# A fused attention and feed-forward kernel: weights fetched four pieces ahead, the first masks moved to ScalarE and POOL, the audit paused and then doubled

## The chip, the cores and the metric

The kernel runs on one NeuronCore of a Trainium2 chip. Its engines work side by side, each through its own queue in order: TensorE (PE; PEld is its weight load) multiplies matrices into PSUM, VectorE (DVE) and ScalarE (ACT) work on elements, POOL (GpSimd) does a few set-up operations, and SyncE (SP) issues the DMAs. Times are device microseconds; the metric is the median of the runs.

## The reference

Gated linear attention feeds a two-layer feed-forward net with SiLU:

```
state = alpha[t] * state + k[t] (outer) v[t]      # per batch and head, 48 x 48
y[t]  = q[t] @ state                              # batch 4, heads 8, 768 tokens, head width 48
x     = y as (3072 tokens, 384)
h     = x @ w_in ; g = h * sigmoid(h)             # w_in: 384 x 2048
out   = g @ w_out                                 # w_out: 2048 x 384
```

q, k, v and alpha are float32. The two weights come as float64, so the kernel turns them into float32 itself.

## The kernel before

**Attention by chunks.** The 768 tokens of each batch are cut into 6 chunks of 128; with 4 batches these are 24 chunks, NT. A chunk n passes four stages. `products(n)` brings alpha, k and q into the layout (head width, token), forms by a scan the running products u of alpha, and with them the scaled keys kp; `quotient` makes the reciprocals and, by a second scan, the scaled queries qp. `scores(n)` multiplies kp with qp into two PSUM tiles and multiplies them with a causal mask into g (line 749). `values(n)` multiplies g with v and adds the part of the carried state; `states(n)` updates the state. A step of the main loop runs scores, values and states of chunk n-1 and products of chunk n, in four slots. The first NA = 8 chunks are turned by TensorE transposes (line 683) and use spare buffers; later ones are loaded in blocks and turned by VectorE.

**In the first 8 chunks and after.** The two 64-token halves of a chunk are handled apart: the second half of the heads has its halves swapped in kp (line 700) and in v (`load_v`, three DMAs a chunk), and scores are made in 16 small matmuls. All 24 chunks do this, though only the later ones leave out the empty quarter of the causal triangle.

**Weights.** `weights(which)` is a generator. A piece is 128 rows by 512 columns of w_in (12 pieces) or by 384 of w_out (16 pieces). `fetch` DMAs the 64-bit numbers into one of four buffers `bits`; ScalarE makes the low word's rounding `up` (line 613), and three VectorE instructions (616, 617, 618) assemble the float32. `convert` is called as the feed-forward work comes near. Before, three pieces are fetched at the very start (`load_w(3)`), the others when they are converted.

**Feed-forward.** Work is cut into `pieces` that `fill` puts between the attention's slots by a table of costs and due times. `enter_plain` (line 839, groups 0 and 1) and `enter` (line 862) make g from x, `leave` (line 960; the very first in line 987) makes the output from g. From group 2 on sums of blocks stand for some of the products, and VectorE makes these sums: `sums_w` of the weights, `sums_x` of the tokens, and those on g in `enter` (line 876).

**The audit.** The fast path holds only where alpha and the weights lie within bounds. `audit` is a generator: 37 times (9 pieces of alpha, 28 of the weights) it loads a piece into the single buffer `look` (lines 643, 645) and, when it is called next, reduces it on VectorE (line 653). Before, `fill` calls it once a step from step 8 on; those left over run after the loop, with one or two feed-forward pieces between them. Then a one-column matmul (line 1179) joins the bounds, and its result `small` decides whether the general path must run. Further pieces of output work follow it.

**Queues.** The tile framework puts each engine's instructions in an order by its own scheduling and adds semaphores. PSUM for attention (`ps_a`) has three buffers. In the first chunks k and q are transposed into the banks of the output work (`ps_o`).

Of the kernel before, what the change touches and what calls it, by code (L numbers as in the profile page):

```python
# [9 lines left out]
I32 = mybir.dt.int32  # L10
U32 = mybir.dt.uint32
U8 = mybir.dt.uint8
AF = mybir.ActivationFunctionType
# [342 lines left out]
def quotients(  # L356
# [58 lines left out]
    def out_bank(i, n):  # L415
        return outs[i].tile([128, 512], F32, name="ps_o")[:, 0:n]
# [58 lines left out]
    def load_v(n):  # L475
        c = ctxs.setdefault(n, dict(zip(("ci", "b"), divmod(n, B))))
        x = v[c["b"], :, c["ci"] * C : c["ci"] * C + C, :].transpose([1, 0, 2])
        t = c["v"] = vns[n % NV]
        nc.sync.dma_start(t[:, 0 : H // 2, 0:D], x[:, 0 : H // 2])
        for e in range(2):  # L480
            nc.sync.dma_start(t[CH * e : CH * e + CH, H // 2 :, 0:D], x[CH - CH * e : C - CH * e, H // 2 :])

    early = []
    wide = moe_w_in.dtype != F32

    def fetch(src):
        n = src.shape[1]
        bits = raw.tile([128, 512, 2], I32, name="bits")[:, 0:n, :]
        nc.sync.dma_start(bits.rearrange("p n w -> p (n w)"), src.bitcast(I32))
        return bits  # L490

    def load_w(n):

        for _ in range(n if wide else 0):
            t = len(early)
            early.append(fetch(moe_w_in[t * 128 : t * 128 + 128, 0:512]))

    load(0)
    load(1)
    load_w(3)  # L500

# [46 lines left out]

        return quads[:, at // NKT, at % NKT] if at < 4 * NKT else late["wx"][:, at - 4 * NKT]

    for n in range(2, NIN):
        load(n)
    for n in range(NV):
        load_v(n)

    def combine(to, sa, a, sb, b):
        if sa == sb == 1:
# [33 lines left out]
    def weights(which):  # L593

        pieces = [
            (w_in[:, t, c : c + 512], moe_w_in[t * 128 : t * 128 + 128, c : c + 512])
            for c in range(0, DF, 512) for t in range(NKT)  # L600
        ] if which == 0 else [
            (w_out[:, f, :], moe_w_out[f * 128 : f * 128 + 128, :]) for f in range(NFT)]
        for dst, src in pieces:
            if not wide:
                act.dma_start(dst, src)
                yield
                continue
            n = dst.shape[1]
            bits = early.pop(0) if which == 0 and early else fetch(src)
            lo, hi = bits.bitcast(U32)[:, :, 0], bits[:, :, 1]  # L610
            up = upp.tile([128, 512], I32, name="up")[:, 0:n]

            tc.keep_in_program_order(act.activation(up, lo, AF.Copy, scale=2.0**-29))
            w = dst.bitcast(I32)
# [3 lines left out]
            dve.tensor_tensor(w, w, up, ALU.add)  # L618
            yield


# [40 lines left out]
    def turned(x, to):  # L662
        x = x[:, 32:].rearrange("p (g j d) -> p g j d", j=4, d=D)
        dve.transpose(to.rearrange("p g (b j) -> p g j b", j=4), x[:, :, :, 0:32])

    def products(n):

        c = ctxs[n]
        sg = seg[0 if late else n % 2]
        ps = {}  # L670

        for name in ("a", "k", "q"):
            if n >= NA:
                if name == "a":
                    turned(c[name], tokens(sg))
                continue
            if n < GB and name != "a":

                ps[name] = out_bank("kq".index(name), 512).rearrange("p (j c) -> p j c", c=C)
            else:  # L680
                ps[name] = ps_attn()
            for j in range(NP):
                pe.transpose(ps[name][:, j, :], c[name][:, 2 * j : 2 * j + 2, :], ident)
            if name == "a":
                act.copy(tokens(sg), ps[name])
        end = NP * W
        u = upool.tile([128, end + 1], F32, name="u")
        dve.tensor_tensor_scan(u[:, end - 1 :: -1], sg[:, end:0:-1], one[:, end:0:-1],  # L688
                               0.0, ALU.mult, ALU.add)

        dve.tensor_single_scalar(least[:, n, :], u[:, 0:end:W], 2.0**-64, ALU.max)  # L691
        kp = c["kp"] = turns(kps, n)
        ut = tokens(u)
        if n >= NA:
            ps["k"] = late["turn"].tile([128, NP, C], F32, name="turn")
            turned(c["k"], ps["k"])
        j = NP // 2
        dve.tensor_tensor(kp[:, 0:j], ps["k"][:, 0:j], ut[:, 0:j], ALU.mult)
        k, ut = [x[:, j:].rearrange("p j (e c) -> p j e c", e=2) for x in (ps["k"], ut)]
        dve.tensor_tensor(kp[:, j:].rearrange("p j (e c) -> p j e c", e=2)[:, :, ::-1], k, ut, ALU.mult)  # L700
        if n >= NA:
            c["sg"] = sg
        else:
            quotient(n, sg, ps["q"])

    def quotient(n, sg=None, q=None):

# [24 lines left out]
    def scores(n):  # L732
        c = ctxs[n]
        ci, b = c["ci"], c["b"]
        ps = c.pop("blank") if n >= NA else [ps_attn() for _ in range(2)]

        for j in (0, 2, 1, 3):
            for e in range(2):  # L740
                for u in range(2):
                    r = slice(64 * u, 64 * u + D)
                    at = slice(CH * e, CH * e + CH)
                    t = slice(CH * (e ^ j // 2) if n >= NA else 0, C)
                    pe.matmul(ps[u][at, j, t], lhsT=c["kp"][r, j, at], rhs=c["qp"][r, j, t],  # L745
                              start=True, stop=True)
        g = c["g"] = work.tile([128, 2, NP, C], F32, name="g")
        for u in range(2):
            dve.tensor_tensor(g[:, u].rearrange("p (o j) c -> p o j c", o=2),  # L749
                              ps[u].rearrange("p (o j) c -> p o j c", o=2),  # L750
                              mask[:, :, None, :].to_broadcast([128, 2, NP // 2, C]), ALU.mult)
# [365 lines left out]
    def fill(step, slot):  # L1117

        at = step * SLOTS + slot
        if at < marks[0]:  # L1120
            if step >= 1:
                convert(0, (at - SLOTS) * 3 // (marks[0] - SLOTS) + 1)
            return
        i = next(i for i, m in enumerate(marks[1:]) if at < m)
        a, b = [work_at[n] for n in ([0] + phases)[i : i + 2]]
        due = a + (b - a) * (at - marks[i] + 1) / (marks[i + 1] - marks[i])
        if late and at % 4 == 0:
            next(audits, None)
        while work_at[done + 1] <= due and pieces[done][2] <= bridged:
            convert(0, 3 * (done // 2) + 6)  # L1130
            convert(1, 3 * (done - 6) // 2)
            go_on()

    for step in range(STEPS):
        stages = [[(scores, 1)], [(products, 0)], [(values, 1)], [(states, 1)]]
        if step < GB:

            stages = stages[1::-1] + stages[2:]
        elif step >= NA:
            stages = [[(scores, 1)], [(products, 0)], [(values, 1), (states, 1)], [(quotient, 0), (blank, 0)]]  # L1140
# [32 lines left out]
        dve.tensor_single_scalar(e, e, bound, holds)  # L1173
    good = work.tile([128, 1], F32, name="good")
    dve.tensor_reduce(good, ends, axis=AX, op=ALU.min)  # L1175
    go_on()
    go_on()
    ps = ps_attn()[0:1, 0, 0:1]
    pe.matmul(ps, lhsT=good, rhs=mask[:, 0, C - 1 : C], start=True, stop=True)  # L1179
    dve.tensor_single_scalar(small, ps, 127.5, ALU.is_ge)  # L1180
# [62 lines left out]
```

## Time and profile before

| | us |
|---|---|
| median of 10 runs | 571.14 |
| lowest and highest | 569.85, 573.98 |
| the profiled execution | 572.79 |
| its span | 571.0 |
| TensorE busy | 553.1 |
| VectorE busy | 448.8 |
| ScalarE busy | 202.0 |
| POOL busy | 8.4 |

| row of the profile | count | mean ns |
|---|---|---|
| mask product, VectorE, line 749 | 48 | 684 |
| scans, VectorE, lines 688 and 716 | 24 each | 1210, 1228 |
| key products, halves, lines 698 and 700 | 24 each | 414 to 424 |
| a w_in piece on VectorE, lines 616 to 618 | 12 each | 420, 685, 689 |
| rounding of a piece, ScalarE, line 613 | 28 | 611 |
| audit reductions, VectorE, line 653 | 65 | 687 |

The span runs from the program's first instruction to its last. A busy TensorE is not TensorE at its peak, since matmuls are pipelined and their ends are modelled. Every tile name is the program's own; `out<-in` says what an instruction writes and reads. Float32 matmuls show as two records each. Where idle time stands before an instruction, the name after the arrow is what ended it.

### The profile page before, as it was taken

The page shows a single profiled execution, that of the slowest core. Times are in us where ns is not written, and L with a number is a line of the kernel's source. Part 1 is how long each engine was busy: PE and PEld are TensorE (multiplying, and loading weights), DVE is VectorE, ACT ScalarE, POOL GpSimd, SP SyncE. Part 2 cuts the span into 40 slices and gives each one's busy share as a digit, 9 for nine tenths or more (in the row PEclk, how much of TensorE's full clock was granted, in tenths as well). Part 3 has the DMA queues.
Part 4 walks back from the last instruction along what each step waited for, and adds up shares of the span by engine and source line. Part 5 has one row for each costly group of instructions (what it writes and reads, how often), then busy time and mean ns, then how long its engine had stood idle before and what let it go on. Part 6 is the DMA issues. An engine that isn't in the chain of part 4 may idle for free. (4 is left out here: it accounts for less than half of the span.)

```text
span 571.0 us, 12612 instructions
## 1 busy us (share of the span) xinstructions
PE 553.1 (97%) x5154; PEld 489.8 (86%) x5154; DVE 448.8 (79%) x831; ACT 202.0 (35%) x399; POOL 8.4 (1%) x28
## 2 busy tenths in 40 slices
PE   5899999999999999899999999999999999999986
PEld 4677887678999999799999999999898999998986
DVE  5779698489798799996898897898894866757651
ACT  2336543133331342452443453443443241423100
POOL 4000000100000000000000000000000000000000
PEclk9899999999999999899999999999999999999999
DMA  9997682344434433433424423425410113333320
GB/s 213 164 294 186 198 207 72 95 104 121 121 100 123 111 104 95 133 82 97 127 50 123 125 71 104 126 49 128 127 39 22 52 58 115 115 103 119 104 71 27
DMA packets 94675, 63.83 MB, mean 112 GB/s; under 512 B 55568, under 2 KB 86288, under 8 KB 94608
## 3 DMA queue, kind: packets, MB, share of 16 engines
q1 hardware_dynamic: 94608, 62.94, 42.0%
q8 instruction: 42, 0.69, 0.5%
q14 instruction: 25, 0.20, 0.1%
HBM read 58.20 MB, written 4.72 MB: 110 GB/s over the span
## 5 line engine op out<-in xcount | busy, mean ns | idle before, releaser
L960 PE MATMUL ps_o<-w_out,g 128*128 128x192 f32 x704 | 122.7, 328 | 0.9 <-DVE o L974 0.8
L960 PEld LDWEIGHTS ps_o<-w_out,g 128*128 128x128 f32 x704 | 115.3, 190 | 3.8 <-DVE o L974 1.4
L960 PE MATMUL ps_o<-wt,g 128*128 128x192 f32 x528 | 91.6, 327 | 0.3 <-DVE u L1036 0.3
L839 PE MATMUL ps_m<-xt,w_in 128*128 128x256 f32 x384 | 88.9, 383 | 0.3 <-DVE w_in L618 0.3
L960 PEld LDWEIGHTS ps_o<-wt,g 128*128 128x128 f32 x528 | 87.2, 191 | 1.9 <-DVE u L1036 0.6
L839 PEld LDWEIGHTS ps_m<-xt,w_in 128*128 128x128 f32 x384 | 71.1, 190 | 10.9 <-DVE w_in L618 1.1
L862 PE MATMUL ps_m<-xc,w_in 128*128 128x256 f32 x288 | 70.1, 380 | 1.2 <-DVE g L876 1.2
L653 DVE TENSOR_REDUCE seen<-bits 128x1 f32<-128x384 int32 (+2 forms) x65 | 42.4, 687 | 25.6 <-DMA bits<-in_moe_w_out_dram 20.2
L862 PEld LDWEIGHTS ps_m<-xc,w_in 128*128 128x128 f32 x288 | 54.1, 191 | 7.6 <-DVE g L876 1.5
L873 ACT ACTIVATE g<-g 128x1024 f32<-128x1024 f32 x32 | 33.2, 1056 | 60.8 <-DVE g L876 60.8
L868 ACT COPY g<-ps_m 128x512 f32<-128x512 f32 x64 | 37.0, 585 | 38.2 <-PE ps_m L862 38.2
L862 PE MATMUL ps_m<-xc,wx 128*128 128x256 f32 x192 | 50.2, 384 | 0.0
L965 DVE TENSOR_TENSOR g<-g 128x512 f32<-128x512 f32 x66 | 44.3, 688 | 2.9 <-PE ps_o L960 2.9
L876 DVE TENSOR_TENSOR g<-ps_m,g 128x512 f32<-128x512 f32 x56 | 37.7, 684 | 2.5 <-PE ps_m L862 2.2
L761 ACT ACTIVATE st<-st,least 128x96 f32<-128x96 f32 x80 | 24.1, 364 | 44.1 <-DVE least L691 44.1
L749 DVE TENSOR_TENSOR g<-ps_a,mask 128x512 f32<-128x512 f32 x48 | 31.2, 684 | 9.4 <-PE ps_a L745 9.0
L862 PEld LDWEIGHTS ps_m<-xc,wx 128*128 128x128 f32 x192 | 35.0, 190 | 4.1 <-issue 0.4
L842 ACT ACTIVATE g<-ps_m 128x512 f32<-128x512 f32 x32 | 19.1, 595 | 47.9 <-PE ps_m L839 47.7
L688 DVE TENSOR_TENSOR_SCAN u<-al,one 128x516 f32<-128x516 f32 x24 | 29.0, 1210 | 8.2 <-POOL mask L529 4.5
L716 DVE TENSOR_TENSOR_SCAN p<-al,inv 128x516 f32<-128x516 f32 x24 | 29.5, 1228 | 6.8 <-PE ps_a L781 6.6
L781 PE MATMUL ps_a<-g,vn 128*32 128x128 f32 x768 | 29.6, 286 | 0.0
L781 PEld LDWEIGHTS ps_a<-g,vn 128*32 128x32 f32 x768 | 21.3, 114 | 8.8 <-issue 6.6
(121 smaller groups left out, 649.0 us busy)
## 6 DMA issues: line engine op xcount, KB each, us to landing
bits<-in_moe_w_in_dram SPq DMA_DIRECT2D x24, 512.0 KB, 4.1
bits<-in_moe_w_out_dram SPq DMA_DIRECT2D x32, 384.0 KB, 3.1
at<-in_alpha_dram SPq DMA_DIRECT2D x64, 96.0 KB, 2.3
kt<-in_k_dram SPq DMA_DIRECT2D x64, 96.0 KB, 2.4
qt<-in_q_dram SPq DMA_DIRECT2D x64, 96.0 KB, 2.4
bits<-in_alpha_dram SPq DMA_DIRECT2D x9, 512.0 KB, 3.4
out_dram<-o SPq DMA_DIRECT2D x48, 96.0 KB, 2.0
vn<-in_v_dram SPq DMA_DIRECT2D x24, 96.0 KB, 2.9
```

Source lines behind the costliest of these rows:

```text
L653: dve.tensor_reduce(seen[kind][which][:, i : i + 1], x, axis=AX, op=op, apply_absolute_value=True))
L688: dve.tensor_tensor_scan(u[:, end - 1 :: -1], sg[:, end:0:-1], one[:, end:0:-1], 0.0, ALU.mult, ALU.add)
L716: dve.tensor_tensor_scan(p[:, 0:end], sg[:, 0:end], iv[:, 0:end], 0.0, ALU.mult, ALU.add)
L749: dve.tensor_tensor(g[:, u].rearrange("p (o j) c -> p o j c", o=2), ps[u].rearrange("p (o j) c -> p o j c", o=2), mask[:, :, None, :].to_b ...
L781: pe.matmul(py[32 * at : 32 * at + 32, t, :], lhsT=w, rhs=x, start=(i < 4), stop=(i >= len(todo) - 4), skip_group_check=True)
L839: pe.matmul(ps[:, e, :], lhsT=w_in[:, t, (f + e) * 128 : (f + e + 1) * 128], rhs=xt[:, t, :], start=(t == 0), stop=(t == NKT - 1))
L862: pe.matmul(ps[:, e], lhsT=block_w(w)[:, 2 * pair + e], rhs=block_x(grp, x), start=(first and e == 0), stop=(e == 1), skip_group_check=True)
L868: act.copy(to, ps)
L873: act.activation(x, x, AF.Silu)
L876: dve.tensor_tensor(to, a, b, op)
L960: pe.matmul(ps, lhsT=x, rhs=w[:, i], start=(first and i == 0), stop=(i == HF - 1), skip_group_check=True)
L965: dve.tensor_tensor(cells(grp, h, pair, *to), cells(grp, h, pair, *x), cells(grp, h, pair, *y), ALU.subtract)
```

## The change

The first 8 chunks no longer swap their halves: one v DMA, one key product over all heads, 8 score matmuls of full width instead of 16 of half width. For the first 4 chunks (GB) ScalarE copies the scores from PSUM and POOL applies the causal mask in place; chunks 4 to 7 keep the VectorE mask. Chunk 1's k and q are transposed into banks of the feed-forward work (`bank`) rather than `ps_o`.

Weights are fetched in one list, w_in and then w_out: four pieces at the start, with chunk 0's and 1's v between them, and one more after each conversion, so that four are always under way. ScalarE's rounding of the next piece is issued right after the three VectorE instructions of the present one. Only in step 1 do the products come before the scores; before it was in steps 0 to 3. Loads of the next chunks move to the end of `states`.

The audit starts at step 15 and is called in two of the four slots of each step. After it, five pieces of output work are issued instead of two ahead of the one-column matmul, and four behind it as before.

```diff
@@ load_v
+        if n < NA:
+            nc.sync.dma_start(t[:, :, 0:D], x)
+            return
         nc.sync.dma_start(t[:, 0 : H // 2, 0:D], x[:, 0 : H // 2])
...
+    pieces_in = [(t, c) for c in range(0, DF, 512) for t in range(NKT)]
+    sources = [moe_w_in[t * 128 : t * 128 + 128, c : c + 512] for t, c in pieces_in]
+    sources += [moe_w_out[f * 128 : f * 128 + 128, :] for f in range(NFT)]
+    coming = []
+
+    def fetch():
+        if wide and sources:
+            src = sources.pop(0)
+            n = src.shape[1]
+            bits = raw.tile([128, 512, 2], I32, name="bits")[:, 0:n, :]
+            nc.sync.dma_start(bits.rearrange("p n w -> p (n w)"), src.bitcast(I32))
+            coming.append(bits)
 
     load(0)
     load(1)
-    load_w(3)
+    for i in range(4):
+        fetch()
+        if i % 2 == 0:
+            load_v(i // 2)
...
-    for n in range(2, NIN):
-        load(n)
-    for n in range(NV):
-        load_v(n)
@@ weights
+        def rounding(bits):
+            n = bits.shape[1]
+            up = upp.tile([128, 512], I32, name="up")[:, 0:n]
+            tc.keep_in_program_order(
+                act.activation(up, bits.bitcast(U32)[:, :, 0], AF.Copy, scale=2.0**-29))
+            return up
+
+        ahead = []
+        for i, (dst, src) in enumerate(pieces):
...
-            bits = early.pop(0) if which == 0 and early else fetch(src)
-            tc.keep_in_program_order(act.activation(up, lo, AF.Copy, scale=2.0**-29))
+            bits = coming.pop(0)
+            up = ahead.pop() if ahead else rounding(bits)
...
             dve.tensor_tensor(w, w, up, ALU.add)
+            if i + 1 < len(pieces):
+                ahead.append(rounding(coming[0]))
+            fetch()
             yield
@@ products
-                ps[name] = out_bank("kq".index(name), 512).rearrange("p (j c) -> p j c", c=C)
+                at = "kq".index(name)
+                ps[name] = (bank(at) if n == 1 else out_bank(at, 512)).rearrange("p (j c) -> p j c", c=C)
...
+        if n < NA:
+            dve.tensor_tensor(kp, ps["k"], ut, ALU.mult)
+            quotient(n, sg, ps["q"])
+            return
@@ scores
-            for e in range(2):
+            for e in range(2 if n >= NA else 1):
                 for u in range(2):
                     r = slice(64 * u, 64 * u + D)
-                    at = slice(CH * e, CH * e + CH)
+                    at = slice(CH * e, CH * e + CH) if n >= NA else slice(0, C)
...
         for u in range(2):
+            if n < GB:
+                act.copy(g[:, u], ps[u])
+                gps.affine_select(g[:, u], g[:, u], pattern=[[0, NP], [1, C]], compare_op=ALU.is_ge,
+                                  fill=0.0, base=0, channel_multiplier=-1)
+                continue
+            m = mask[:, :, None, :] if n >= NA else mask[:, 0:1, None, :]
@@ fill
-        if late and at % 4 == 0:
+        if at % 2 == 0 and step > 3 * GB + 2:
             next(audits, None)
@@ main loop
+        if step == 1:
+            load(NIN)
         stages = [[(scores, 1)], [(products, 0)], [(values, 1)], [(states, 1)]]
-        if step < GB:
+        if step == 1:
             stages = stages[1::-1] + stages[2:]
...
-                if stage is products and n + NIN < NA:
-                    load(n + NIN)
+                if stage is states and n + 1 + NIN < NA:
+                    load(n + 1 + NIN)
@@ after the loop
-    go_on()
-    go_on()
+    for _ in range(5):
+        go_on()
     ps = ps_attn()[0:1, 0, 0:1]
     pe.matmul(ps, lhsT=good, rhs=mask[:, 0, C - 1 : C], start=True, stop=True)
```

More of the change, by code (lines that the diff above doesn't have):

```diff
@@ L481, in load_v @@
             nc.sync.dma_start(t[CH * e : CH * e + CH, H // 2 :, 0:D], x[CH - CH * e : C - CH * e, H // 2 :])
-    early = []
     wide = moe_w_in.dtype != F32
[L486 to L496, printed above, removed]
+    pieces_in = [(t, c) for c in range(0, DF, 512) for t in range(NKT)]
[9 more added lines that the diff above has]
+            coming.append(bits)
     load(0)
     load(1)
-    load_w(3)
+    for i in range(4):
+        fetch()
+        if i % 2 == 0:
+            load_v(i // 2)
     seg = [(fix if i == 0 else spare).tile([128, NP * W + 1], F32, name=f"al{i}") for i in range(2)]
@@ L599, in weights @@
             (w_in[:, t, c : c + 512], moe_w_in[t * 128 : t * 128 + 128, c : c + 512])
-            for c in range(0, DF, 512) for t in range(NKT)
+            for t, c in pieces_in
         ] if which == 0 else [
             (w_out[:, f, :], moe_w_out[f * 128 : f * 128 + 128, :]) for f in range(NFT)]
-        for dst, src in pieces:
+        def rounding(bits):
[6 more added lines that the diff above has]
+        for i, (dst, src) in enumerate(pieces):
             if not wide:
@@ L607, in weights @@
                 continue
-            n = dst.shape[1]
-            bits = early.pop(0) if which == 0 and early else fetch(src)
-            lo, hi = bits.bitcast(U32)[:, :, 0], bits[:, :, 1]
-            up = upp.tile([128, 512], I32, name="up")[:, 0:n]
-            tc.keep_in_program_order(act.activation(up, lo, AF.Copy, scale=2.0**-29))
-            w = dst.bitcast(I32)
+            assert which == 0 or conv_done[0] == n_conv[0]
+            bits = coming.pop(0)
+            up = ahead.pop() if ahead else rounding(bits)
+            hi, w = bits[:, :, 1], dst.bitcast(I32)
             tc.keep_in_program_order(
@@ L700, in products @@
         dve.tensor_tensor(kp[:, j:].rearrange("p j (e c) -> p j e c", e=2)[:, :, ::-1], k, ut, ALU.mult)
[L701 to L704, printed above, removed]
+        c["sg"] = sg
     def quotient(n, sg=None, q=None):
@@ L748, in scores @@
         for u in range(2):
+            if n < GB:
[4 more added lines that the diff above has]
+            m = mask[:, :, None, :] if n >= NA else mask[:, 0:1, None, :]
             dve.tensor_tensor(g[:, u].rearrange("p (o j) c -> p o j c", o=2),
                               ps[u].rearrange("p (o j) c -> p o j c", o=2),
-                              mask[:, :, None, :].to_broadcast([128, 2, NP // 2, C]), ALU.mult)
+                              m.to_broadcast([128, 2, NP // 2, C]), ALU.mult)
         if ci < NCH - 1:
```

## The prediction

> **What bounds the kernel now.** I read the page's first two parts, then the busy time by stretch, then the timeline at the stretches where TensorE is not full. Columns of the first line: busy us, share, instructions; of the rows below it: tenths in 40 slices of 14.3 us.
>
> ```profile
> PE 553.1 (97%) x5154; PEld 489.8 (86%) x5154; DVE 448.8 (79%) x831; ACT 202.0 (35%) x399; POOL 8.4 (1%) x28
> PE   5899999999999999899999999999999999999986
> DVE  5779698489798799996898897898894866757651
> PEclk9899999999999999899999999999999999999999
> DMA  9997682344434433433424423425410113333320
> ```
>
> TensorE is the bound: from slice 3 on it is full but for a dent in slice 17 and the end. So only three places can give time back: the start, the dent, the end. Busy time by stretch (us, TensorE, its weight loads, VectorE, ScalarE, POOL, granted clock, DMA):
>
> ```profile
> 10.00:15.00 5.00, 3.69 (x40) 2.97 (x40) 4.86 (x10) 0.68 (x1) 0.00 (x0) 1.00 1.18 314
> 20.00:25.00 5.00, 3.57 (x64) 2.57 (x59) 4.93 (x10) 0.70 (x2) 0.00 (x0) 0.89 0.79 127
> 25.00:30.00 5.00, 5.00 (x49) 3.96 (x46) 2.37 (x4) 1.67 (x4) 0.00 (x0) 0.77 1.18 262
> 200.00:250.00 50.00, 48.36 (x460) 43.60 (x459) 48.79 (x94) 19.17 (x38) 0.00 (x0) 0.97 0.39 107
> 350.00:400.00 50.00, 50.00 (x487) 45.92 (x476) 44.62 (x80) 20.70 (x42) 0.00 (x0) 1.00 0.37 97
> 540.00:550.00 10.00, 8.46 (x50) 7.71 (x48) 4.59 (x15) 0.32 (x1) 0.00 (x0) 1.00 0.39 111
> ```
>
> In the start VectorE is nearly full while TensorE has holes and a low clock. In 200 to 250 VectorE has 1.2 us left of 50 and TensorE loses 1.64 us and 3% of its clock. The timeline at these places (start, length, engine):
>
> ```profile
> 23.48 0.41 PE L683 MATMUL ps_o<-ident,kn 128*128 128x128 f32 x2 [1.43 <-DMA kn<-in_k_dram]
> 28.82 5.45 PE L839 MATMUL ps_m<-xt,w_in 128*128 128x256 f32 x24
> 35.37 0.70 PE L839 MATMUL ps_m<-xt,w_in 128*128 128x256 f32 x2 [0.30 <-DVE w_in L618]
> ...
> 232.41 1.21 DVE L653 TENSOR_REDUCE seen<-bits 128x1 f32<-128x1024 f32 x1
> 237.07 1.13 PE L862 MATMUL ps_m<-xc,w_in 128*128 128x256 f32 x4 [1.24 <-DVE g L876]
> ...
> 550.31 0.19 PE L1179 MATMUL ps_a<-mask,good 128*1 128x1 f32 x2 [1.57 <-DVE good L1175]
> ```
>
> The first feed-forward matmul starts at 28.82: chunk 3's transposes stand ahead of it in TensorE's queue and waited 1.43 us for k, which stood behind earlier loads. The last waits are those on an audit: its 1.21 us reduction is in VectorE's queue just ahead of the sums that the matmul at 237.07 waits for, and the one-column matmul at 550.31 waits for the last audit's verdict.
>
> [...]
>
> **The start.** Removed from VectorE: 8 mask products of 0.684 (chunks 0 to 3), 5.5 us, and for 8 chunks two key products of 0.42 become one of 0.69, 1.2 us. Added: 8 ScalarE copies of 0.585, 4.7 us, on an engine that is 35% busy, and 8 POOL selects of 128x512. The page has selects of 128 columns at 0.29; memsets of 128 and 517 columns take 0.20 and 0.53. By the memset's slope a select is 0.61; four short ones would be 1.17. I take 0.9[...]; both ends go into the range. Score matmuls: 16 on quarters of the array become 8 on halves. The old 32 records take about 0.85 us, four side by side; two side by side come to the same 0.85, one at a time would be 1.7. I take no change. SP issues one v load for three (16 fewer in the 8 chunks, about 0.6 us each), hidden behind DMA that is full.
>
> DMA lands in the order of issue (landing times of the trace): a chunk's 192 KB load takes 1.2 us, a 512 KB weight piece 1.3. The first six loads land as before, at 9.88. Then piece 0 11.2, v0 12.4, pieces 1 and 2 13.7 and 15.0, v1 16.2, piece 3 17.5, chunk 2's loads 21.1.
>
> VectorE: chunk 0 from 5.88 for 4.2 us (two scans of 1.23, two products of 0.69, two short ones of 0.17), chunk 1 to 14.0, pieces 0 to 2 behind them at 1.75 each. ScalarE has piece 1's rounding queued ahead of chunk 0's copies, so these wait for the landing at 13.7: rounding to 14.4, copies to 15.6, selects to 16.9, values to 18.2, then their copy out, and because PSUM has three buffers, chunk 1's scores only at 18.9, at half clock to 20.6. Chunk 1's copies, its k copy and the rounding of piece 3 stand ahead of chunk 2's alpha copy, which ends near 23.8. The first feed-forward matmul follows at about 26.0, with three chunks transposed instead of four (1.3 us): at equal work 28.8 against 27.3.
>
> The rest of the gain comes after it: VectorE does chunk 2 (4.2) to 28.0 and pieces 3 to 5 to 33.4, where TensorE, after 12 matmuls of 0.427 and chunk 2's scores, waits about 0.5; chunk 3 and pieces 6 to 11 end near 48.3, where they ended at 55.9. TensorE's first 48 feed-forward matmuls then end near 53.9; before, the same work ended near 59.0. That is 5.1 us. I take off 0.6 for switches of 0.2 to 0.3 between kinds of matmul[...]. **3.5 us**, from 0 to 5.5. Chunks 4 and 5 are loaded later than before, behind weights, near 37 and 50; they are wanted after 50 and 65.
>
> **The middle.** Audits leave steps 8 to 14, seven of 1.21 us. VectorE had no idle gap over 0.25 us from 198 to 241 and ran two audits in it, 2.4 us; TensorE's waits there were 1.24 and 0.40. Without them both waits go, and the low clock with them: 1.64 idle + 0.03 x 50 = 3.1. TensorE's order there is the same. **2.9 us**, from 1 to 3.1.
>
> **Two audits a step** from step 15, ten steps: ten more audits before the tail at 1.21 to 1.36 each. A step is 22 us; in 350 to 400 VectorE has 5.4 us free of 50, 2.4 a step, so 1.3 fits. The second falls in the slot of states and values, where VectorE has gaps of 2.15 and 0.95 in every other step. In the other (sums of the tokens) it has none for 20 us. On SP an audit's transfer waits for the reduction before it (5.8 us at most in the trace), and the next chunk's loads and the stores stand behind it; the loads have about 20 us until they are wanted. The 12.1 us that SP waited at 94 for the first audit's buffer go: hidden either way. **-0.7 us**, from 0 to -3.
>
> **The end.** 37 audits less 20 leaves 17, where 20 were left. Each takes 4.15 there (3.3 for the transfer into the one buffer, 1.0 for its reductions), so the verdict comes 12.5 us earlier. The one-column matmul is followed by 64 output matmuls, not 46; eight take 2.6, so TensorE comes to it 5.9 us earlier. The wait of 1.57 goes, with 6 us to spare. **1.7 us**, from 1.5 to 2.5 (a 0.29 wait on an audit at 545 may go too).
>
> **Sum.** 3.5 + 2.9 - 0.7 + 1.7 = 7.4. The profiled execution took 572.79, 571.0 of it span; it becomes 565.4 with a span of 563.6. The median shown, 571.14, lies 1.65 below that execution: 571.14 - 7.4 = **563.7**.
>
> **Rivals.** [...] The start gains nothing: 571.1 - 3.9 = 567.2. Second, the stall at 237 was not the audits' but the weight sums': it stays or moves on; 571.1 - 3.5 - 1.7 + 0.7 = 566.6. For it: some two dozen of them at 0.42 fill the same 43 us. Third, on the other side: two audits a step make the stall of 237 in the steps from 15 on. One costs 3.1 us, as there; the other parts gain 8.1, so from three of the ten steps the kernel is slower; at four, 571.1 - 8.1 + 12.4 = 575.4. Against it: 350 to 400 lost nothing at 44.62 of 50, and 1.3 a step makes that 47.6, still under 48.79.
>
> **Chances.** The forecast 0.61, first rival 0.17, second 0.12, third 0.10. A measurement of this kernel tells about 0.2%, 1.1 us, from no change. Faster 0.87, same 0.03 (the first two together), slower 0.10. Low end: 5.5 + 3.1 + 2.5 without crowding is 11.1, too much at once; 559.5. High end: past the first two rivals, 569.5, leaving out the third.
>
> **What would show it.** Right: first feed-forward matmul near 26, last w_in piece near 48; 200 to 250 with TensorE at 50.0 and clock 1.00; no wait before the one-column matmul; VectorE at 47 to 48 in 350 to 400. Wrong: selects well over 1.2 us, or VectorE pieces waiting on POOL; feed-forward matmuls waiting on w_in beyond 1 us; TensorE idle over 1 us between 330 and 520, which would speak for the third rival.

## The result and the profile after

The changed kernel has a median of 564.18 us (563.61 to 565.78, 9 runs); the kernel before has 571.17 (31 runs). The ratio is 0.9876, with a 95% interval of 0.9863 to 0.9889. Run again on another chip, beside the experiments, it had 565.47 against 574.0, ratio 0.9865 (0.9832 to 0.9897). The forecast was 563.7 with a range of 559.5 to 569.5: the time lies 0.5 us above the forecast.

The page of the changed kernel, its first two parts, answers to the lines shown of before:

```profile
PE 548.4 (98%) x5026; PEld 488.8 (87%) x5026; DVE 445.5 (79%) x815; ACT 205.3 (37%) x407; POOL 14.8 (3%) x36
PE   6899999999999999999999999999999999999995
DVE  5797898488798599986998897899895875856731
PEclk9999999999999999999999999999999999999999
```

The dent of TensorE in slice 17 is gone, and so is the drop of its clock there. In slice 2 no drop is shown either, but what these views say of the clock ahead of 19 us is no measurement, as the experiments show. Busy time by stretch (TensorE, weight loads, VectorE, ScalarE, POOL, granted clock, DMA):

```profile
10.00:15.00 5.00, 3.96 (x24) 3.00 (x23) 4.79 (x9) 2.11 (x4) 0.22 (x1) 1.00 1.13 320
20.00:25.00 5.00, 4.76 (x85) 3.28 (x83) 2.43 (x4) 3.38 (x9) 1.22 (x2) 1.00 1.09 275
25.00:30.00 5.00, 4.92 (x23) 4.07 (x24) 4.76 (x9) 2.40 (x6) 0.00 (x0) 1.00 0.92 211
200.00:250.00 50.00, 49.88 (x507) 45.60 (x507) 47.57 (x90) 21.33 (x44) 0.00 (x0) 1.00 0.31 80
350.00:400.00 50.00, 50.00 (x473) 45.60 (x472) 46.89 (x90) 20.57 (x41) 0.00 (x0) 1.00 0.43 118
540.00:550.00 10.00, 10.00 (x63) 10.00 (x63) 4.83 (x8) 0.95 (x3) 0.00 (x0) 1.00 0.05 15
```

In 200 to 250 TensorE now has 49.88 of 50 at full clock, with VectorE at 47.57, and 540 to 550 is full. In 10 to 15 it has 3.96 of 5 where it was 3.69. The timeline of TensorE at the places that the prediction named:

```profile
15.75 0.64 PE L801 MATMUL ps_a<-g,vn 128*32 128x128 f32 x4 [1.79 <-POOL g L765]
25.09 2.86 PE L859 MATMUL ps_m<-xt,w_in 128*128 128x256 f32 x12 [0.26 <-ACT xt L806]
232.62 1.13 PE L882 MATMUL ps_m<-xt,w_in 128*128 128x256 f32 x4
535.46 0.19 PE L1201 MATMUL ps_a<-mask,good 128*1 128x1 f32 x2
```

The first feed-forward matmul starts at 25.09 instead of 28.82. The matmul that waited 1.24 us near 237 has its counterpart at 232.62 and waits for nothing that is shown, and neither does the one-column matmul at 535.46. New is the 1.79 us that TensorE waits for chunk 0's masked scores.

**Where the time went.** TensorE's order of work after the start is the same in both kernels, so the same event can be compared at several points. I take ScalarE's copy of a chunk's values into xt, for chunk 12 (start done), 14 (first step after the stretch without audits) and 23 (all steps done), and the end of the span. Times are us in the profiled executions; "gain" is against before at that point, "share" what the stretch since the last point adds.

| | before | after | gain | share | predicted |
|---|---|---|---|---|---|
| chunk 12 | 218.38 | 214.19 | 4.19 | start 4.2 | 3.5 |
| chunk 14 | 264.88 | 257.29 | 7.59 | middle 3.4 | 2.9 |
| chunk 23 | 454.17 | 447.48 | 6.69 | two audits a step -0.9 | -0.7 |
| end of the span | 571.05 | 562.37 | 8.68 | end 2.0 | 1.7 |

The shares add up to 8.7, the medians differ by 7.0. The profiled execution of before took 572.79 and lies 1.6 above its median, that of after (564.11) at its median; in which stretch a usual execution of before is that much better, one profile cannot tell. Among the executions of the kernel before that stand beside the experiments, the longer ones have the lower mean granted clock (572.2 us at 0.998, 577.6 us at 0.990).

### The profile page after: what moved, and what is told of

It is laid out like the page before. It is cut to its first block, busy times and chain, and to the rows that moved or that the text cites. A ratio compares the mean times of both kernels' runs of the same rounds, so it can differ in the third digit from the quotient of the medians.

```text
span 562.4 us, 12315 instructions
## 1 busy us (share of the span) xinstructions
PE 548.4 (98%) x5026; PEld 488.8 (87%) x5026; DVE 445.5 (79%) x815; ACT 205.3 (37%) x407; POOL 14.8 (3%) x36
## 4 chain that ended last, share of the span: by engine, by line
PE 76%; DVE 13%; DMA 5%; SPq 1%; ACT 1%; issue 1%; POOL 0%; DVEq 0%; ACTq 0%
PE ps_o L980 28%; PE ps_m L882 17%; PE ps_m L859 14%; PE ps_a L801 6%; PE ps_o L1007 4%; PE ps_a L758 3%; DMA bits<-in_moe_w_out_dram 3%; DVE seen L664 2%; DVE g L896 2%; PE ps_a L775 1%; DVE turn L675 1%; DMA bits<-in_moe_w_in_dram 1%; PE ps_a L695 1%; PE ps_a L816 1%; DVE g L985 1%
## 5 line engine op out<-in xcount | busy, mean ns | idle before, releaser
L769 DVE TENSOR_TENSOR g<-ps_a,mask 128x512 f32<-128x512 f32 x40 | 25.7, 685 | 8.9 <-PE ps_a L758 8.6
L801 PE MATMUL ps_a<-g,vn 128*32 128x128 f32 x768 | 28.4, 282 | 2.1 <-POOL g L765 2.0
```

What stands on the lines that cost most here:

```text
L801: pe.matmul(py[32 * at : 32 * at + 32, t, :], lhsT=w, rhs=x, start=(i < 4), stop=(i >= len(todo) - 4), skip_group_check=True)
```

## The experiments

The same table for every run ("the ledger" below), all against the profiled execution of before, in us (a minus is a loss). The second column is the time in the span from which TensorE has its full clock for good in the start; before has 27.32 there.

| run | full clock from | start | middle | steps 15 to 24 | end | ratio to before (95%) |
|---|---|---|---|---|---|---|
| changed kernel again | 19.44 | 3.9 | 3.5 | -0.9 | 2.1 | 0.9865 (0.9832 to 0.9897) |
| old start, new audit | 19.34 | 0.5 | 3.4 | -1.2 | 1.5 | 0.9888 (0.9860 to 0.9917) |
| new start, old audit | 20.07 | 3.7 | 0.0 | 0.0 | -1.5 | 0.9948 (0.9918 to 0.9977) |
| audit from step 8 | 20.13 | 3.6 | 0.0 | -0.5 | 2.7 | 0.9875 (0.9844 to 0.9907) |
| two pieces ahead of the verdict | 20.11 | 3.6 | 3.4 | -0.9 | -0.7 | 0.9912 (0.9880 to 0.9945) |
| no audits in the loop | 21.40 | 3.0 | 3.5 | 0.0 | 1.8 | 0.9848 (0.9817 to 0.9878) |
| masks on VectorE | 26.09 | 1.3 | 3.5 | -0.9 | 1.7 | 0.9892 (0.9862 to 0.9922) |
| products first in steps 0 to 3 | 21.20 | 0.6 | 3.4 | -0.9 | 1.9 | 0.9912 (0.9880 to 0.9945) |
| every rounding late | 12.45 | 5.5 | 3.5 | -0.9 | 1.6 | 0.9822 (0.9799 to 0.9845) |
| second rounding late | 17.61 | 5.1 | 3.4 | -0.9 | 1.6 | 0.9823 (0.9799 to 0.9848) |
| audit with a gap | 20.60 | 3.4 | 2.6 | -0.9 | 3.5 | 0.9843 (0.9819 to 0.9866) |
| late rounding and gap | 11.06 | 5.2 | 3.4 | -0.9 | 1.6 | 0.9818 (0.9790 to 0.9845) |

The start of one and the same code differs by up to 1.2 us between executions (3.0 to 4.2 in the seven kernels that start like the changed one); the middle and the steps 15 to 24 repeat to 0.1 us where their code is the same, the end to 0.5. The kernel before had medians of 573.3 to 574.7 on the chips of the experiments.

**Where the start's spread comes from.** The trace of each run lists the stretches of granted clock, full or half. In every run this list begins some time into the span with a stretch of full clock, and the views count the time ahead of it as 1.00. TensorE is in fact at half speed there: in the changed kernel's first profile the list begins at 19.01, and four transposes take 1.11 us at 12.84, 213 ns apart, and 0.66 us at 20.39, 109 ns apart. Where a stretch of half clock lies inside the list, the view shows it, as in the changed kernel's second profile (half from 16.03 to 19.44, third number from the end):

```profile
15.00:20.00 5.00, 3.77 (x73) 3.28 (x75) 4.46 (x7) 1.92 (x5) 1.90 (x2) 0.66 1.33 233
```

In the seven kernels that start like the changed one the start's share follows this time: full clock for good from 19.01, 19.44, 20.07, 20.11, 20.13, 20.60 and 21.40 goes with shares of 4.2, 3.9, 3.7, 3.6, 3.6, 3.4 and 3.0. A microsecond later costs half a microsecond (1.2 over 2.4 us), as half speed would. So starts can be compared only at a like clock, and some kernels below have it far from the others.

### The start and the audit apart

Old start, new audit:

```diff
--- before
-        if late and at % 4 == 0:
+        if at % 2 == 0 and step > 3 * GB + 2:
             next(audits, None)
...
-    go_on()
-    go_on()
+    for _ in range(5):
+        go_on()
```

> The kernel before with only the changed audit (from step 15, two a step) and five output pieces ahead of the one-column matmul; the start stays as it was. Theory (the gain is start 4.2, middle 2.7, crowding -0.2, end 2.0 by the equal-work points of the two traces): middle, crowding and end come, the start does not: 571.2 - 4.5 = 566.7, or up to 568 if the dent at 237 was larger in the profiled execution of before than usual. First feed-forward matmul stays near 28.8. Rival 'the stall at 237 belongs to the weight sums': it stays, and only the end comes, 569.4. Rival 'two audits a step make new stalls': 571 or more.

Measured: 568.36 where before had 573.74. Middle and end came without the new start (3.4 and 1.5), and the crowding was a little more (-1.2). Its start is that of before, and the 0.5 is within what executions of one start differ by. The stall of 237 is gone while the weight sums stay.

New start, old audit:

```diff
--- after
-        if at % 2 == 0 and step > 3 * GB + 2:
+        if late and at % 4 == 0:
             next(audits, None)
...
-    for _ in range(5):
-        go_on()
+    go_on()
+    go_on()
```

> The changed kernel with the audit of before (one a step from step 8) and two output pieces ahead of the one-column matmul; only the start is new. Theory: the start's 4.2 us come alone, 567.0; the stall near 233 to 237 and a wait of about 1.6 before the one-column matmul are back in the profile. Rival '[...] start gains nothing': 571. If the two halves add up, its gain and that of the kernel with the old start make 7.0 together.

Measured: 570.99, 2.75 below before; the start's gain is there at chunk 12 (3.7) and still there at chunk 23. Then 1.5 are lost at the end, where output work waits 1.50 us near 523 and the one-column matmul 1.67. The median alone, 570.99, is the rival's 571, but before has 573.74 on this chip, and the ledger puts the shortfall at the end. So rival one, "the start gains nothing", falls. The two halves do not quite add up by medians: 5.4 and 2.75 make 8.1 against the 7.0 of the first comparison and the 8.5 of the second; the intervals (about 1.7 each) cover both.

### The stall near 237

```diff
--- after
-        if at % 2 == 0 and step > 3 * GB + 2:
+        if late and at % (2 if step > 3 * GB + 2 else 4) == 0:
             next(audits, None)
```

> The changed kernel with one audit a step in steps 8 to 14 as before, two a step from 15; so seven fewer are left for the end. Theory: two audits lie in 193 to 237 again, VectorE is full there, the stall at 237 is back and with it the dent of the clock: 565.5 to 566.9, and the gain over before at the stage of 240 to 260 falls by 1.5 to 2.7 us. Rival 'weight sums make the stall, not the audits': TensorE keeps 49.9 of 50 us in 200 to 250, time 564.2.

The stall is back to the hundredth, and nothing else in that stretch was changed. Timeline of this kernel, the reduction on VectorE and what TensorE then waits for:

```profile
228.82 1.21 DVE L664 TENSOR_REDUCE seen<-bits 128x1 f32<-128x1024 f32 x1
233.48 1.13 PE L882 MATMUL ps_m<-xc,w_in 128*128 128x256 f32 x4 [1.24 <-DVE g L896]
235.02 1.96 PE L882 MATMUL ps_m<-xt,w_in 128*128 128x256 f32 x4 [0.41 <-DVE g L896]
```

and its stretch of 200 to 250:

```profile
200.00:250.00 50.00, 48.35 (x489) 43.35 (x488) 47.82 (x90) 19.86 (x41) 0.00 (x0) 0.97 0.39 102
```

The waits of 1.24 and 0.41 us are those of before, and the four matmuls after them take 1.96 instead of 1.13: TensorE has slowed. The trace lists half clock from 235.17 to 238.58, 3.41 us, which costs 1.7; with the waits this makes the 3.4 of the ledger, more than the 1.5 to 2.7 expected. The second rival, "the weight sums make the stall", falls: they are in both kernels. The time, 567.06, misses the theory's upper end by 0.2, and the ratio, 0.9875, cannot be told from the changed kernel's: 0.9865. What the middle loses (3.4) comes back in part: the steps give up 0.5 instead of 0.9, for a reason that no run shows, and the end, with seven audits fewer left, brings 2.7 instead of 2.0.

```diff
--- after
-        if at % 2 == 0 and step > 3 * GB + 2:
+        if late and at % (2 if step > 3 * GB + 2 else 4) == 0 and step not in (11, 12, 13):
             next(audits, None)
```

> The changed kernel with one audit a step in steps 8 to 10 and 14, none in 11 to 13, two a step from 15; four fewer are left for the end. Theory (only the stretch 193 to 241 has no room on VectorE, and the end's audits cost VectorE-bound waits of 0.3 to 0.6 near 484 and 520): no stall near 233 to 237 if no reduction falls between 198 and 237; the waits of the end shrink by 0.4; 563.8 where the changed kernel has 564.2. Rival 'any audit before step 15 makes the stall': TensorE loses 2 us near 233 to 237, 566.

Measured: 564.36, and neither side as put. One reduction did fall into the stretch. The timeline:

```profile
228.06 1.21 DVE L664 TENSOR_REDUCE seen<-bits 128x1 f32<-128x1024 f32 x1
232.72 1.13 PE L882 MATMUL ps_m<-xc,w_in 128*128 128x256 f32 x4 [0.26 <-DVE g L896]
234.25 1.13 PE L882 MATMUL ps_m<-xt,w_in 128*128 128x256 f32 x4 [0.40 <-DVE g L896]
```

One audit in the stretch costs 0.26 and 0.40 us of waiting with the matmuls still at full speed (the trace lists no half clock there), 0.8 in the ledger; two cost 3.4. This fits a lateness that adds up because VectorE cannot work it off between 198 and 237, and it grows more than in proportion because the longer waits are followed by the 3.41 us of half clock. The end brought 3.5, 1.5 more than in the changed kernel: none of the waits near 483 and 520 is there, as expected of fewer audits, but by more than expected.

### Two audits a step

```diff
--- after
+        todo = todo[:1] + todo[-16:]
         for kind in (0, 1):
...
-        if at % 2 == 0 and step > 3 * GB + 2:
+        if False:
             next(audits, None)
```

> The changed kernel with none of the 20 audits of steps 15 to 24: those 20 pieces of alpha and w_in are not audited at all; the 17 of the end stay. Theory (crowding as the prediction priced it, 0.7): from the 15th to the 24th chunk the changed kernel gives back 0.9 us against before at equal work; without audits there it gives back nothing, and the time is 0.7 to 0.9 us lower than the changed kernel's, 563.4 where that has 564.2. Rival 'the small losses there are the new phase of the steps, not the audits': no difference. Rival 'each of them costs a stall of 3 us': 560 or less.

Measured: 564.91 beside 565.47 for the changed kernel, a difference inside both intervals; the profiled execution had a start 1 us worse, with full clock 2.0 us later. By the ledger it is plain: 0.0 instead of -0.9 between chunks 14 and 23. Busy time in 270 to 460, first of the changed kernel run beside it, then of this one:

```profile
270.00:460.00 190.00, 189.67 (x1808) 173.72 (x1808) 169.16 (x300) 75.90 (x144) 0.00 (x0) 1.00 0.41 110
```

```profile
270.00:460.00 190.00, 190.00 (x1814) 174.50 (x1813) 150.15 (x267) 76.57 (x144) 0.00 (x0) 1.00 0.23 57
```

VectorE falls by 19 us, and the third of a us that TensorE was idle goes; the rest of the 0.9 must lie in small delays that TensorE's row shows as busy. The third rival, a stall of 3 us in several of the ten steps, falls. That one audit a step cost nothing there follows too: before had one a step, this kernel has none, and the share is 0.0.

### The end

```diff
--- after
-    for _ in range(5):
-        go_on()
+    go_on()
+    go_on()
     ps = ps_attn()[0:1, 0, 0:1]
```

> The changed kernel with two output pieces ahead of the one-column matmul instead of five; 17 audits are left for the end as in the changed kernel. In its trace the verdict is ready at 531.3 and the matmul runs at 535.5; three pieces of 2.6 us fewer in front bring TensorE to it at 527.7. Theory: it waits 3.6 us, time 567.8, so the five pieces and not the fewer audits take the wait away. Rival 'three audits fewer at the end take it away, with 6 us to spare' (as the prediction worked it out): a wait of 1.8 at most, 564.2 to 566.

Timeline of this kernel:

```profile
532.56 0.16 DVE L1197 TENSOR_REDUCE good<-ends 128x1 f32<-128x4 f32 x1
532.77 0.19 PE L1201 MATMUL ps_a<-mask,good 128*1 128x1 f32 x2 [2.08 <-DVE good L1197]
```

The wait is 2.08 us with 17 audits left and two pieces ahead; before it was 1.57 with 20 left and two ahead. The median is 568.2, 0.4 above what was expected, though the wait itself is 1.5 shorter than expected: the end's share falls by 2.7, of which 2.1 is this wait and the rest are longer waits near 484, 520 and 542. So the five pieces take the wait away. Fewer audits do not do it by themselves, because each audit of the end carries one or two pieces with it: the verdict and the matmul that needs it move together.

### The masks

```diff
--- after
         for u in range(2):
-            if n < GB:
-
-                act.copy(g[:, u], ps[u])
-                gps.affine_select(g[:, u], g[:, u], pattern=[[0, NP], [1, C]], compare_op=ALU.is_ge,
-                                  fill=0.0, base=0, channel_multiplier=-1)
-                continue
```

> The changed kernel with the masks of chunks 0 to 3 on VectorE (one product of 128x512 for each half, as chunks 4 to 7 have it); no ScalarE copy, no POOL select. Theory (the masks are in VectorE's way): 8 x 0.685 = 5.5 us more on VectorE before 45; chunk 0's and 1's masks go into its idle 2.5 us near 21, chunk 2's push w_in's pieces 3 to 5 from 32.8 to about 34.5, and TensorE waits there 1.5 to 2 us: 565.7 to 566.2 where the changed kernel has 564.2. Rival '[...] the move gains nothing': 564.2, or 563 since values of chunk 0 then start about 1 us sooner.

Measured: 567.58, 2.1 above the changed kernel beside it and 2.6 at chunk 12. The direction is the theory's, the mechanism is not: no feed-forward matmul waits for w_in. Of the 2.6, 2.1 are there when the first feed-forward matmul starts (27.48 against 25.35 beside it). TensorE ran at half speed nearly up to then (full clock from 26.09). The same work, chunk 1's scores and transposes, in the changed kernel, with chunk 0's transposes ahead of them:

```profile
12.84 1.11 PE L775 MATMUL ps_a<-ident,kp 128*128 128x128 f32 x4
19.18 1.26 PE L758 MATMUL ps_a<-p,kp 48*128 48x128 f32 x16
20.39 0.66 PE L775 MATMUL ps_a<-ident,kp 128*128 128x128 f32 x4
```

and with the masks on VectorE (two of the score records come earlier):

```profile
19.24 2.07 PE L758 MATMUL ps_a<-p,kp 48*128 48x128 f32 x14
21.25 1.11 PE L769 MATMUL ps_a<-ident,kp 128*128 128x128 f32 x4
```

Its stretch of 20 to 25, with the granted clock third from the end:

```profile
20.00:25.00 5.00, 5.00 (x30) 4.06 (x27) 2.81 (x5) 2.15 (x4) 0.00 (x0) 1.00 1.14 281
```

Transposes follow one another 213 ns apart here and 109 ns apart there. The 1.00 is no grant: the trace's list begins only at 26.09, just where the spacing halves. In the changed kernel TensorE works from 15.75 with one hole of 0.24 us, and full clock comes at 19.01, 3.3 us later. In this kernel TensorE shows no hole from 16.67 on, and full clock comes 9.4 us later.

This is enough for the whole loss. By the half microsecond for each microsecond of the seven kernels above, full clock at 26.09 would leave a start of about 0.6 (an estimate); the share is 1.3, and chunk 0's values start sooner, at 14.21 instead of 15.92 beside it. So that masks on VectorE are in the way is not shown. The median of six executions is 2.1 higher, though the two intervals overlap; whether the masks on VectorE bring the full clock late, or it came late by chance, stays open.

### The order of products and scores

```diff
--- after
-        if step == 1:
+        if step < GB:
 
             stages = stages[1::-1] + stages[2:]
```

> The changed kernel with products ahead of scores in steps 0 to 3, as before, instead of in step 1 alone. This puts chunk 2's transposes ahead of chunk 1's scores in TensorE's queue, and chunk 3's ahead of chunk 2's scores. Theory (the order, not the masks, brings the first feed-forward matmul forward): chunk 1's scores and values wait for chunk 2's loads, which land at 18.7 to 20.9, the first feed-forward matmul comes 1 to 2 us later than at 25.1, and so does all that follows: 565.2 to 566.2. Rival 'the order is worth nothing, the loads set it': 564.2.

Measured: 568.4, 2.9 above the changed kernel beside it; 3.3 at chunk 12, more than expected. About 1 us of this is the clock: the kernel without audits in the loop, which has almost the same list (half from 14.57 to 21.40, here from 14.38 to 21.20), starts its feed-forward work at 26.32 and has a start of 3.0, so that 2.4 remain for the order. Timeline of TensorE:

```profile
25.09 0.41 PE L801 MATMUL ps_a<-g,vn 128*32 128x128 f32 x4 [0.70 <-POOL g L765]
27.33 5.45 PE L859 MATMUL ps_m<-xt,w_in 128*128 128x256 f32 x24 [0.24 <-ACT xt L806]
42.64 1.07 PE L801 MATMUL ps_a<-g,vn 128*32 128x128 f32 x28 [1.35 <-POOL g L765]
```

Chunk 1's values start at 25.09, when the changed kernel already does feed-forward work, and the first such matmul comes 2.0 us later than in the changed kernel beside it, 1.0 later than in the one with the like clock. A second loss is at 42.64, where values follow their scores so closely that TensorE waits 1.35 us for the ScalarE copy and the select: only work between scores and values hides the way over ScalarE and POOL, and with this order there is none. So the new order is worth about 2.4 of the start beside the masks on POOL. What fetching four pieces ahead, the undivided key product and the full-width scores are worth by themselves, no run tells.

### The rounding one piece ahead

```diff
--- after
-            if i + 1 < len(pieces):
-                ahead.append(rounding(coming[0]))
             fetch()
```

> The changed kernel with every piece's rounding issued with its own three VectorE instructions, as before, not one piece ahead. On ScalarE chunk 0's copies then stand ahead of piece 1's rounding. Theory (the 1.8 to 3.6 us that TensorE waits for chunk 0's select come from copies queued behind a rounding that waits for piece 1's landing): values of chunk 0 start near 14.2 instead of 15.75 to 16.0, the first feed-forward matmul near 23.7, and the kernel is 1.0 to 1.5 us faster than the changed one. Rival 'rounding ahead is what keeps the pieces on time': VectorE waits for roundings, pieces 3 to 5 come late, and it is 1 us or more slower than the changed kernel.

Timeline of this kernel, ScalarE, POOL and TensorE:

```profile
12.89 1.07 ACT L762 COPY g<-ps_a 128x512 f32<-128x512 f32 x2 [0.76 <-PE ps_a L756]
13.55 1.22 POOL L763 TENSOR_SCALAR_AFFINE_SELECT g<-g 128x512 f32<-128x512 f32 x2 [6.54 <-ACT g L762]
14.23 0.41 PE L799 MATMUL ps_a<-g,vn 128*32 128x128 f32 x4 [0.79 <-POOL g L763]
23.79 2.86 PE L857 MATMUL ps_m<-xt,w_in 128*128 128x256 f32 x12 [0.26 <-ACT xt L804]
```

The same of the changed kernel:

```profile
13.57 0.66 ACT L610 ACTIVATE up<-bits 128x512 int32<-128x512 uint32 x1 [1.65 <-DMA bits<-in_moe_w_in_dram]
14.14 1.05 ACT L764 COPY g<-ps_a 128x512 f32<-128x512 f32 x2
14.78 1.95 POOL L765 TENSOR_SCALAR_AFFINE_SELECT g<-g 128x512 f32<-128x512 f32 x2 [7.77 <-ACT g L764]
```

In the changed kernel ScalarE stood 1.65 us at piece 1's landing with chunk 0's copies queued behind it. With the rounding late, the copies start when the scores are there, the values at 14.23 and the first feed-forward matmul at 23.79, as the theory had it. Time 563.33, ratio 0.9822; on this chip the kernel with the audit gap, which starts like the changed one, had 564.36. So rounding one piece ahead costs about 1 us by the medians. How much of that is the waiting alone stays open, since full clock comes at 12.45 here and at 19.01 in the changed kernel.

```diff
--- after
-            if i + 1 < len(pieces):
+            if 0 < i and i + 1 < len(pieces):
                 ahead.append(rounding(coming[0]))
```

> The changed kernel with only piece 1's rounding issued with its own VectorE instructions; all others stay one piece ahead. TensorE's and VectorE's orders are those of the changed kernel. Theory: as with all roundings late, 1.0 to 1.5 us faster than the changed kernel, and if rounding ahead is worth anything later, a little faster than with all late. Rival 'chunk 2's loads, landing at 18.7 to 20.9, and w_in's pieces 3 to 5 set the feed-forward work, not chunk 0': no gain over the changed kernel.

Measured: 563.18, ratio 0.9823: by the medians this one rounding is the whole gain, and since the shares after the start are those of the kernel with all roundings late, rounding ahead is worth nothing measurable later. Chunk 0's values start at 14.53. Of the 0.9 gained at chunk 12 over the changed kernel, up to 0.7 can be the clock (full from 17.61 instead of 19.01, at half a microsecond each); whether the earlier work brought it earlier, no run tells.

The two findings together, late rounding and an audit without steps 11 to 14 (the two diffs above, with 14 added to the list):

> The kernel with every rounding issued with its own VectorE instructions (0.9822 of the kernel before), and besides one audit a step in steps 8 to 10, none in 11 to 14, two a step from 15; three fewer are left for the end. Theory: reductions fall at about 126 and 145 and then after 245, so the stall near 232 stays away (TensorE 49.8 of 50 in 200 to 250), the start keeps its 1.3 us over the changed kernel, and the waits of the end near 484 and 520 shrink or go: 0.5 to 1.5 us faster than with the late rounding alone, 0.9795 to 0.9813 of the kernel before. Rival 'the end does not depend on how many audits are left': 0.982.

Measured: 563.51 (0.9818): the start and the middle are as expected, the end is not better, and the ratio misses the theory's 0.9795 to 0.9813. The waits near 483 are gone, but the joining of the bounds now falls into VectorE's queue where output work needs it:

```profile
518.76 0.15 DVE L1195 TENSOR_REDUCE good<-ends 128x1 f32<-128x4 f32 x1
...
518.90 0.59 PE L978 MATMUL ps_o<-w_out,g 128*128 128x192 f32 x2 [1.05 <-DVE good L1195]
```

It seems that the end depends on what happens to lie beside the audits at least as much as on how many are left. The three versions with late rounding have the lowest times of all, 563.2 to 563.5, and cannot be told from each other. Against the changed kernel they gain about 1 us: on one chip the first two had times of 563.0 to 564.2 where the kernel with the audit gap had 564.0 to 564.8.

## Why the prediction was right

**Start (3.5; measured 4.2, and 3.0 to 3.9 in other executions).** The hand schedule held. Landings came within 0.2 us of it, the rounding of piece 1 ahead of chunk 0's copies did make TensorE wait (copies to 15.2 where 15.6 was worked out), the last w_in piece ended at 48.3 as predicted, and the 48 matmuls at about 54.3 (53.9). The first feed-forward matmul was 0.9 us earlier than the 26.0 given, because chunk 1's scores and chunk 2's transposes ran at full speed from 19.0 on where half speed was assumed to 20.6. That was luck: in other executions of the same start full speed came as late as 21.40, and that matmul between 25.35 and 26.32. The 0.5 us wait on pieces 3 to 5 did not come. Of the start's edits only three were taken back alone, so which of them bring the gain is shown in part: the order of products and scores brings 2.4, the masks' part is open, and rounding ahead, which the sum gave no price of its own, costs about 1.

**The selects beside VectorE (1.0 taken off).** Of the 5.1 worked out for the start 0.6 went for switches; the other 1.0, for selects that slow a full VectorE, was an estimate that no trace of before showed. POOL and VectorE do slow each other, but off the path. Two selects beside w_in pieces (14.78, above) took 1.95; two beside an idle VectorE (21.08, changed kernel) took 1.22, and so did two with a VectorE product from PSUM beside the first (13.55, every rounding late). VectorE's side in the changed kernel:

```profile
15.34 0.90 DVE L626 CUSTOM_DVE_ANT_0 w_in<-w_in,up 128x1024 uint16<-128x1024 uint16 x1
16.16 0.85 DVE L624 TENSOR_SCALAR w_in<-bits 128x512 int32<-128x512 int32 x1
```

These take 0.69 and 0.42 at 17.87 and 18.48 of the same trace. It need not be both that are slowed: with every rounding late two selects kept their 1.22, and the VectorE instruction beside the second (14.26) took 0.79 instead of 0.42. In the changed kernel chunks 0 and 2 lose VectorE 0.6 and 0.5 us, chunk 1 nothing, where the masks of one chunk would take 1.37 (two of 0.684); no feed-forward matmul waited for a piece, so the deduction was not needed. What it is in these instructions that makes the two slow each other, no run shows. The select itself is 0.61, the low end by the memset slope, not the 0.9 taken.

**Middle (2.9; measured 3.4).** The mechanism is shown by putting the audits back. The term a little small is the clock: 0.03 x 50 = 1.5 came from a rounded 0.97, while the trace of before lists 3.41 us of half clock from 238.94, which is 1.7; with the waits of 1.64 this makes 3.3. The prediction had 3.1 and then took 2.9 without saying why.

**Two audits a step (-0.7; measured -0.9).** VectorE came to 46.89 in 350 to 400, just under the 47 to 48 given.

**End (1.7; measured 2.0).** The wait is gone. At equal work the verdict came 12.3 us earlier (550.26 to 531.27, less the 6.7 gained by then; 12.5 predicted); the spare was 4.2, not 6; the prediction's own figures give 5.0 (12.5 less 5.9 less 1.57). The possible 0.29 at 545 went too, and output work that waited 0.79 near 526 waits 0.35 and 0.19 in two places. What the sum did not say is which edit did it: the wait stayed with two pieces ahead, and five removed it.

The sum was 0.4 too large against the medians (7.4 to 7.0) and 1.3 too small against the profiled executions (8.7). The profiled execution of before is 1.6 above its median, so part of what its trace shows as lost is not lost in a usual run; that the sum fits the medians better than its own trace is partly luck. The low end of the range, 559.5, lies below what its parts give: 571.1 less 11.1 is 560.0. The first two rivals fell by one run each (new start with old audit, audit from step 8), the third by the kernel without loop audits.

## What to carry to other kernels

Work put "ahead" on an in-order engine is ahead of everything behind it too: one rounding that waited 1.65 us for a DMA, with the first chunk's copies behind it in the queue, went with a loss of about 1 us. Housekeeping belongs where its engine has slack for it: one reduction in a full stretch cost 0.8 us, two 3.4, and twenty in the looser steps 0.9. To account for a change, compare one and the same event in both traces at several points; in the later stages here it repeats to a tenth of a microsecond where the code is the same, which the medians of a noisy baseline do not. In the start it does so only at a like clock: look for the moment of full speed first, by the spacing of like matmuls or the trace's list.

## What the runs showed that was not expected

- TensorE's half speed lasted 9.4 us of work without a recorded hole (masks on VectorE: no hole from 16.67 on, transposes still 213 ns apart at 21.25, full clock from 26.09). In the changed kernel's first profile full clock came 3.3 us after chunk 0's values began (15.75 to 19.01).
- A granted clock of 1.00 in a view of the first microseconds can mean that the trace lists nothing there. In the kernel before and in the changed one transposes follow one another 213 ns apart ahead of the list's first entry (at 17.07 and 19.01) and 109 ns apart after it.
- The moment differs between executions of one program: the changed kernel had full clock for good from 19.01 in one, and in another from 12.62 to 16.03 and then again from 19.44. This accounts for the spread of the start; what sets the moment, no run shows.
- Waits of 1.24 and 0.41 us close together were followed by 3.41 us of half clock, waits of 0.26 and 0.40 were not; nor was a single wait of 2.08 (two pieces ahead of the verdict).
- In the changed kernel a 128x512 float32 select on POOL takes 0.61 us beside an idle VectorE (21.08) and about 0.97 beside the VectorE instructions of a w_in piece (14.78 and 32.76); these grow from 0.42 to 0.85, from 0.69 to 0.90 and 1.00. A product from PSUM beside a select kept its 0.69 (13.65, every rounding late).
